# Two heads per score matmul and token-major values in a gated mix of linear and local attention

## The chip, the cores and the metric

The kernel runs on one core of a Trainium2 chip. Its time is device time in microseconds (us), and lower is better. The kernel before takes 492.45 us, the median of three runs (492.34 to 493.23). A core has a matrix engine (TensorE, PE in the profile, with its weight loads shown apart as PEld), a vector engine (VectorE, DVE), a scalar engine (ScalarE, ACT), a general engine (GpSimd, POOL) and a queue engine that only issues transfers (SyncE, SP). Matmul results land in PSUM, eight banks of 128 partitions by 512 fp32 columns; all other tiles lie in SBUF.

## The reference, cut to what matters

Sequence length S is 2048, width D is 1024, with 32 heads of 32 dimensions. One input x feeds two attention blocks, A and B, and a gate mixes their outputs.

```
def _A_ref(x, wqkv, wo):                     # linear attention
    phi = lambda t: jnp.where(t > 0, t + 1, jnp.exp(t)) + 1e-6
    pq, pk = phi(q), phi(k)
    kv = einsum("bhsd,bhse->bhde", pk, v);  z = einsum("bhsd->bhd", pk)
    o = einsum("bhqd,bhde->bhqe", pq, kv) / (einsum("bhqd,bhd->bhq", pq, z) + 1e-6)
    return o @ wo
def _B_ref(x, wqkv, wo):                     # local attention
    W, dil = 8, 2                            # each query sees positions s, s-2, ..., s-14
    logits = (q . k at those positions) * Dh ** -0.5, masked below position 0
    o = softmax(logits) weighted sum of v at those positions
    return o @ wo
g = sigmoid((x * gate_w).sum(-1))
out = g * A(x) + (1 - g) * B(x)
```

## The kernel before

Tokens are reordered into even and odd positions (`e_` is 0 or 1, 1024 tokens each, 16 tiles of 128 in all), so that the dilated window of local attention becomes eight neighbouring tokens. All activations are kept feature-major in SBUF: `xT`, `qT` and `kT` are [128, 8, 2048], eight chunks of 128 features, so a chunk `c` holds four heads `j` at 32 partitions each.

The stages, in order of time:

1. Values of B (L1370): each token tile times half of the value weights, token-major; a copy (`move`, on ACT or DVE) puts the 512 columns in a `vst` buffer, and SP writes them to `vB_hbm` in device memory.
2. Keys and queries of B (L1481), first for `e_` = 0, then for `e_` = 1, into `kT` and `qT`. `top` (L1287) keeps a running maximum and minimum of both on DVE.
3. Keys and values of A with the running state (`state`, L1511), token tile by token tile.
4. Queries of A, the state folded into A's output weights (`fold`), denominators (`over`), A's output (`a_out`), and at the end `final` (L1636), which multiplies `qT` (by then holding B's attention output) with B's output weights and mixes.

Local attention is cut into 18 fills, nine for each `e_`. A fill covers two blocks (`h` is 0 or 1) of 57 queries (56 in the last fill of nine), and each block needs the 64 keys before and at its queries. Fills are put between the projection groups of the second half of stage 2 and of stage 3: `slot` is called after each group, its rate of 0.2 (`FILL`) starts a fill every five groups, and `after(PVLAG, values)` puts the values three slots after the scores. In a fill, with four PSUM banks `SO` of its own:

- SP loads 64 token rows of `vB_hbm` for each block (L1411) into one of three `v` buffers.
- Scores (`s_fn`, L1418): for every chunk, block and head one matmul, 64 in all, with the 64 keys of the head as stationary operand (32 partitions by 64 columns) and 57 queries moving. Head `j` writes bank `j`, block `h` the partitions from 64`h`.
- ACT takes the exponential of all four banks into `E` (L1424), and DVE multiplies by a 0/1 mask (L1427).
- Values (`values`, L1432): for every head and block one matmul, 64 in all, with 64 tokens by 32 value columns as stationary operand and 57 columns of `E` moving; the result is feature-major. After `SUMS_AT` = 3 chunks, eight matmuls with `ones` as stationary operand give every head's sum, repeated over its 32 partitions (L1444).
- For each block ACT takes Ln of the sums (L1453) and the exponential of its negative (L1454), and DVE multiplies the result by it and overwrites the queries in `qT` (L1456).

The order of all instructions is made when the program is built: every `P.op` names its engine, an assumed cost, what it reads and writes, and a priority (its place in the program unless given). `schedule` is a list scheduler that goes through assumed time, gives each engine the ready operation of lowest priority number, and lets an operation marked `any` go to ACT or DVE, whichever would end it first. On PE it also prefers an operation of the same tile `mode` as the last. The result is a fixed order for each engine and for the SP queue, with semaphore waits where one engine needs another.

Of the kernel before, what the change touches and what calls it, by code (L numbers as in the profile page):

```python
# [1115 lines left out]
def build_kernel(nc, A_x, A_wqkv, A_wo, B_x, B_wqkv, B_wo, gate_w, out):  # L1116
# [10 lines left out]
    def SB(shape, dtype, name, at=None):  # L1127
        n = SZ[dtype]
        for d in shape[1:]:
            n *= d  # L1130
        if at is None:
            at = base[0]
            base[0] += (n + 31) // 32 * 32
        uid[0] += 1
        h = nc.alloc_sbuf_tensor_at("%s_%d" % (name, uid[0]), list(shape), dtype, offset=at)
        return Tile("S", h, at, list(shape), dtype)
# [26 lines left out]
            return ps[:, self.i, lo:hi]  # L1163

    banks = [Bank(i) for i in range(8)]
    vB_hbm = nc.dram_tensor("vB_hbm", [S, D], BF16)
    MX = [("M", 0, 1, None)]
    mx_hbm = nc.dram_tensor("mx_hbm", [4, 128], F32)
    rc_hbm = nc.dram_tensor("rc_hbm", [4, H, 4, 512], F32)
# [6 lines left out]
    kT = SB([128, 8, S], BF16, "kT")  # L1176
    ws = [SB([128, 8, 1024], BF16, "w%d" % i) for i in range(4)]
    pq0 = SB([128, 8, 512], BF16, "pq0")
    ones = SB([128, 32], BF16, "ones")
# [3 lines left out]
    msk = [SB([128, 2, n], BF16, "msk%d" % i) for i, (n, _) in enumerate(KINDS)]  # L1183
    eps = SB([128, 1], F32, "eps")
    gwb = SB([128, 1024], BF16, "gwb")
    gt = SB([128, NT], F32, "gt")
# [9 lines left out]
    er = Ring([SB([128, 512], BF16, "e%d" % i) for i in range(3)])  # L1196

    ph = base[0]
    vst = Ring([SB([128, 512], BF16, "vst%d" % i) for i in range(8)])
    top_ = base[0]  # L1200
    base[0] = ph
    Er = Ring([SB([128, 32 * 57], BF16, "E%d" % i) for i in range(2)])
    Lr = Ring([SB([128, 8 * 57], F32, "L%d" % i) for i in range(2)])
    vr = Ring([SB([128, 1024], BF16, "v%d" % i) for i in range(3)])
# [19 lines left out]

    FILL = 0.2
    PVLAG = 3
    SUMS_AT = 3
    WARM = 11
    PASSES = 6
    mm = lambda n: max(n / 2400.0, 0.0267) + 0.0025  # L1230
# [3 lines left out]
    def plan(seen):  # L1234
# [28 lines left out]
        C("pool", lambda e: e.memset(ones[:], 1.0), 0.1, [ones.all()])  # L1263
# [13 lines left out]
        C("pool", lambda e: e.memset(zsel[:], 0.0), 0.3, [zsel.all()])  # L1277

        C("dve", lambda e: e.memset(warm[:, :], 0.0), 0.15, [warm.all()])
        for m in mx[0:2]:  # L1280
            C("dve", lambda e, m=m: e.memset(m[:, :], 0.0), 0.2, [m.all()])

# [87 lines left out]
        for t, half in [(4 * b + i, half) for b in range(NT // 4) for half in range(2) for i in range(4)]:  # L1370
            vt, vs = vst.next()
            xs, xr = x_tile(t)
            bank = main.next()
            w, wr = w_half(0, half)
            step = 2 if t == 0 else 8
            for d in range(0, 8, step):
                o = group(bank, xs, w, [xr, ws[0].part((d, d + step), (half * 512, half * 512 + 512))], d, d + step)
            move(vt[:, :], bank.ap, 512, bank, vt.all())
            P.op("sp", lambda e, t=t, vt=vt, half=half: e.dma_start(vB_hbm[t * 128:(t + 1) * 128, half * 512:half * 512 + 512], vt[:, :]), 0.6, reads=[vt.all()],
                 writes=[hb(t * 128, (t + 1) * 128, half)], chan="vst%d" % vs, lat=0.5, prio=5)  # L1380
            if (t, half) in early:
                load_w(*early[t, half], after=[o])
# [19 lines left out]
        later = []  # L1402
        slot_n = [0]

        def fill(e_, qs, nq, offs):
            t0 = e_ * HS
            k0 = [qs + nq * h - offs[h] for h in range(2)]
            m = msk[KINDS.index((nq, offs))]
            vt, vslot = vr.next()
            for h in range(2):  # L1410
                P.op("sp", lambda e, h=h: e.dma_start(vt[64 * h:64 * h + 64, :], vB_hbm[t0 + k0[h]:t0 + k0[h] + 64, :]), 0.4,  # L1411
                     reads=[hb(t0 + k0[h], t0 + k0[h] + 64, i) for i in range(2)], writes=[vt.all()], chan="v%d_%d" % (vslot, h), lat=0.5)

            def s_fn(e):
                for c in range(8):
                    for h in range(2):
                        for j in range(4):
                            last = e.matmul(SO[j].ap(c * nq, (c + 1) * nq)[64 * h:64 * h + 64, :], kT[32 * j:32 * j + 32, c, t0 + k0[h]:t0 + k0[h] + 64],  # L1418
                                            qT[32 * j:32 * j + 32, c, t0 + qs + h * nq:t0 + qs + (h + 1) * nq], start=True, stop=True, tile_position=(32 * j, 64 * h))
                return last  # L1420
            P.op("pe", s_fn, 0.55, mode="r", reads=[kT.part((0, 8), (t0 + k0[0], t0 + k0[1] + 64)), qT.part((0, 8), (t0 + qs, t0 + qs + 2 * nq))],
                 writes=[s.iv for s in SO], name="S")
            E, _ = Er.next()
            P.op("act", lambda e: e.activation(E[:, 0:32 * nq].rearrange("p (j q) -> p j q", j=4), ps[:, 4:8, 0:8 * nq], ACT.Exp), act(32 * nq),  # L1424
                 reads=[s.iv for s in SO], writes=[E.all()])
            ev = lambda: E[:, 0:32 * nq].rearrange("p (g q) -> p g q", g=16)
            P.op("dve", lambda e: e.tensor_tensor(ev(), ev(), m[:, :, :].rearrange("p r q -> p (r q)")[:, None, :].to_broadcast([128, 16, 2 * nq]), ALU.mult),  # L1427
                 0.15 + 32 * nq / 1920.0, reads=[E.all(), m.all()], writes=[E.all()])

            def values():  # L1430

                def each(e):  # L1432
                    def part(c):
                        for j in range(4):
                            for h in range(2):
                                hd = 4 * c + j
                                last = e.matmul(SO[h].ap(c * nq, (c + 1) * nq)[32 * j:32 * j + 32, :], vt[64 * h:64 * h + 64, hd * 32:hd * 32 + 32],  # L1437
                                                E[64 * h:64 * h + 64, (8 * j + c) * nq:(8 * j + c + 1) * nq], start=True, stop=True, tile_position=(64 * h, 32 * j))
                        return last
                    for c in range(SUMS_AT):  # L1440
                        part(c)
                    for j in range(4):
                        for h in range(2):
                            e.matmul(SO[2 + h].ap(0, 8 * nq)[32 * j:32 * j + 32, :], ones[64 * h:64 * h + 64, :], E[64 * h:64 * h + 64, 8 * j * nq:8 * (j + 1) * nq],  # L1444
                                     start=True, stop=True, tile_position=(64 * h, 32 * j))
                    for c in range(SUMS_AT, 8):
                        last = part(c)
                    return last
                P.op("pe", each, 0.61, mode="c", reads=[vt.all(), ones.all(), E.all()], writes=[s.iv for s in SO], name="PV")
                for h in range(2):  # L1450
                    L, _ = Lr.next()
                    n = 8 * nq
                    P.op("act", lambda e, L=L, h=h: e.activation(L[:, 0:n], SO[2 + h].ap(0, n), ACT.Ln), act(n), reads=[SO[2 + h].iv], writes=[L.all()])  # L1453
                    P.op("act", lambda e, L=L: e.activation(L[:, 0:n], L[:, 0:n], ACT.Exp, scale=-1.0), act(n), reads=[L.all()], writes=[L.all()])  # L1454
                    q0 = t0 + qs + h * nq
                    P.op("dve", lambda e, L=L, h=h, q0=q0: e.tensor_tensor(  # L1456
                        qT[:, :, q0:q0 + nq], SO[h].ap(0, n).rearrange("p (c q) -> p c q", c=8), L[:, 0:n].rearrange("p (c q) -> p c q", c=8), ALU.mult), dps(n),
                        reads=[SO[h].iv, L.all()], writes=[qT.part((0, 8), (q0, q0 + nq))])
            after(PVLAG, values)

        pace = [0.0]

        states = []
# [308 lines left out]
```

## Time and profile before

| what | before |
|---|---|
| median of the runs | 492.45 us |
| the profiled execution, its own time | 492.7 us |
| its span, first to last instruction | 490.9 us |
| PE, DVE, ACT busy | 99%, 56%, 34% of the span |
| PE share of the chain that ended last | 95% |
| scores, all fills (L1418) | 1152 matmuls |
| values and sums, all fills (L1437, L1444) | 1152 and 144 matmuls |
| state (L1519) | 512 matmuls |
| Ln and exponential in a fill (L1453, L1454) | 548 and 584 ns each |
| DVE multiply into `qT` (L1456) | 628 ns each |

A share of busy time is an average over stages. The line of slices cuts the span in 40 equal parts, each digit the busy tenths of one. The chain of waits is followed back from the last instruction to whatever released each step. A line of the timeline gives start, length, engine, line of the kernel, operation, result and operands, tile and operand shape, and count; matmuls overlap, so the length of a group is the time from its first start to its last end. Fills lie between 126 and 312 us.

### The profile page before, as it was taken

What the parts mean: (1) busy time and instruction counts of PE and PEld (TensorE: products, weight loads), DVE (VectorE), ACT (ScalarE), POOL (GpSimd) and SP (SyncE); (2) the same over time, 40 slices, a digit from 0 to 9 for tenths busy, and PEclk for the clock granted to TensorE, in tenths of its full rate; (3) what the DMA queues carried; (4) which work ended last, traced back from release to release, by engine and by line L of the source; (5) the groups of instructions that cost most, each with busy time, mean ns of one, the idle gap of its engine ahead of it and who ended that gap; (6) DMA issues with size and microseconds to landing.
All of it is one profiled execution on the core that took longest, in us unless ns stands there. A gap on an engine that the chain in (4) does not pass through costs nothing.

```text
span 490.9 us, 11427 instructions
## 1 busy us (share of the span) xinstructions
PE 485.7 (99%) x5123; PEld 226.5 (46%) x5123; DVE 274.5 (56%) x487; ACT 166.9 (34%) x287; POOL 5.1 (1%) x27
## 2 busy tenths in 40 slices
PE   8999999999999999999999999999999999999997
PEld 3444444444444444555454454444444444444443
DVE  2121336899677777465555645596865735334434
ACT  2111121212443344665655556355423323010000
POOL 3000000000000000000000000000000000000000
PEclk9999999999999999999999999999999999999999
DMA  8999993222003045211000100501673406101212
GB/s 208 216 197 271 356 366 100 86 87 85 13 24 109 24 127 146 65 28 43 24 24 24 36 12 4 171 3 22 172 193 80 115 13 180 44 23 45 85 68 89
DMA packets 51069, 48.82 MB, mean 99 GB/s; under 512 B 20161, under 2 KB 38977, under 8 KB 51010
## 3 DMA queue, kind: packets, MB, share of 16 engines
q1 hardware_dynamic: 50322, 47.40, 34.9%
q8 instruction: 42, 0.69, 0.6%
q10 hardware_dynamic: 688, 0.59, 0.4%
q14 instruction: 17, 0.14, 0.1%
HBM read 34.34 MB, written 9.44 MB: 89 GB/s over the span
## 4 chain that ended last, share of the span: by engine, by line
PE 95%; SPq 2%; DVE 2%; DMA 1%; issue 0%
PE ps_all L1326 77%; PE ps_all L1647 11%; PE ps_all L1418 2%; PE ps_all L1437 2%; SPq L1300 1%; PE ps_all L1519 1%; DMA w<-in_B_wqkv_dram 1%; PE ps_all L1444 1%; DVE zsel L1561 1%; SPq L1305 1%; PE ps_all L1598 0%; DVE pq L1339 0%; PE ps_all L1571 0%; DVE e L1337 0%; DVE w L1357 0%
## 5 line engine op out<-in xcount | busy, mean ns | idle before, releaser
L1326 PE MATMUL ps_all<-w,xT 128*128 128x512 bf16 x960 | 213.8, 379 | 0.7 <-DMA xT<-in_A_x_dram 0.6
L1326 PE MATMUL ps_all<-xT,w 128*128 128x512 bf16 x768 | 170.7, 379 | 0.0
L1326 PEld LDWEIGHTS ps_all<-w,xT 128*128 128x128 bf16 x960 | 91.1, 98 | 109.8 <-DMA xT<-in_A_x_dram 2.0
L1326 PEld LDWEIGHTS ps_all<-xT,w 128*128 128x128 bf16 x768 | 73.8, 98 | 89.0 <-issue 1.8
L1647 PE MATMUL ps_all<-w,qT 128*128 128x512 bf16 (+1 forms) x264 | 55.6, 373 | 0.0
L1647 PEld LDWEIGHTS ps_all<-w,qT 128*128 128x128 bf16 x264 | 25.8, 98 | 29.7
L1337 DVE TENSOR_SCALAR e<-e 128x512 bf16<-128x512 bf16 x64 | 18.3, 290 | 34.3 <-ACT e L1335 17.1
L1357 DVE CAST vst<-ps_all 128x512 bf16<-128x512 f32 x15 | 10.4, 691 | 44.3 <-PE ps_all L1326 44.3
L1424 ACT ACTIVATE E<-ps_all 128x1824 bf16<-128x1824 f32 (+1 forms) x18 | 30.4, 1687 | 10.1 <-PE ps_all L1418 9.4
L1335 ACT ACTIVATE e<-ps_all 128x512 bf16<-128x512 f32 x32 | 19.1, 597 | 42.8 <-PE ps_all L1326 42.8
L1427 DVE TENSOR_TENSOR E<-E,msk 128x1824 bf16<-128x1824 bf16 (+1 forms) x18 | 19.8, 1102 | 22.4 <-ACT E L1424 22.4
L1651 DVE SCALAR_TENSOR_TENSOR o<-ps_all,gm,xT 128x512 bf16<-128x512 f32 (+1 forms) x25 | 18.0, 728 | 23.2 <-PE ps_all L1647 22.2
L1333 ACT ACTIVATE e<-ps_all 128x512 bf16<-128x512 f32 x32 | 19.1, 597 | 26.6 <-PE ps_all L1326 25.8
L1358 ACT ACTIVATE vst<-ps_all 128x512 bf16<-128x512 f32 x17 | 10.1, 597 | 49.7 <-PE ps_all L1326 45.5
L1287 DVE TENSOR_TENSOR mx<-mx,kT 128x1024 bf16<-128x1024 bf16 x32 | 20.8, 688 | 9.3 <-ACT kT L1358 9.2
L1287 DVE TENSOR_TENSOR mx<-mx,qT 128x1024 bf16<-128x1024 bf16 x32 | 20.8, 686 | 6.9 <-ACT qT L1361 6.7
L1456 DVE TENSOR_TENSOR qT<-ps_all,L 128x456 bf16<-128x456 f32 (+1 forms) x36 | 21.0, 627 | 6.2 <-ACT L L1454 5.0
L1339 DVE SCALAR_TENSOR_TENSOR pk<-ps_all,e 128x512 bf16<-128x512 f32 x32 | 21.9, 688 | 0.7
L1453 ACT ACTIVATE L<-ps_all 128x456 f32<-128x456 f32 (+1 forms) x36 | 17.8, 547 | 12.4 <-PE ps_all L1437 12.4
L1358 ACT ACTIVATE kT<-ps_all 128x512 bf16<-128x512 f32 x16 | 9.6, 597 | 34.5 <-PE ps_all L1326 34.5
L1361 ACT ACTIVATE qT<-ps_all 128x512 bf16<-128x512 f32 x16 | 9.6, 597 | 31.5 <-PE ps_all L1326 31.5
L1614 DVE TENSOR_TENSOR xT<-xT,rb 128x512 bf16<-128x512 bf16 x24 | 16.2, 688 | 6.6 <-DMA rb<-rc_hbm 6.4
(72 smaller groups left out, 285.6 us busy)
## 6 DMA issues: line engine op xcount, KB each, us to landing
rb<-rc_hbm SPq DMA_DIRECT2D x32, 256.0 KB, 4.8
w<-in_A_wqkv_dram SPq DMA_DIRECT2D x6, 1024.0 KB, 9.3
v<-vB_hbm SPq DMA_DIRECT2D x36, 128.0 KB, 2.8
vB_hbm<-vst SPq DMA_DIRECT2D x32, 128.0 KB, 5.9
w<-in_B_wqkv_dram SPq DMA_DIRECT2D x4, 1024.0 KB, 9.5
xn<-in_A_x_dram SPq DMA_DIRECT2D x16, 256.0 KB, 2.8
out_dram<-o SPq DMA_DIRECT2D x15, 256.0 KB, 2.0
w<-in_A_wo_dram SPq DMA_DIRECT2D x8, 256.0 KB, 3.9
```

Source lines behind the costliest of these rows:

```text
L1287: P.op("dve", lambda e, m=m, op=op: e.tensor_tensor(m[:, 0:n], m[:, 0:n], src, op), 0.08 + n / 1920.0, reads=[m.all(), reg], writes=[m.all()],
L1326: last = e.matmul(bank.ap(), lhs(dc), rhs(dc), start=(dc == 0), stop=(dc == 7))
L1333: P.op("act", lambda e: e.activation(e_[:, :], bank.ap(), ACT.Exp), act(512), reads=[bank.iv], writes=[e_.all()])
L1335: P.op("act", lambda e: e.activation(e_[:, :], bank.ap(), ACT.Exp, accum_out=qe[:, col:col + 1]), act(512) + 0.1, reads=[bank.iv], writes= ...
L1337: P.op("dve", lambda e: e.tensor_scalar(e_[:, :], e_[:, :], 1.0, 1e-6, op0=ALU.min, op1=ALU.add), 0.25, reads=[e_.all()], writes=[e_.all()])
L1339: P.op("dve", lambda e: e.scalar_tensor_tensor(out=dst, in0=bank.ap(), scalar=0.0, in1=e_[:, :], op0=ALU.max, op1=ALU.add), dps(512), read ...
L1358: fa = lambda e: e.activation(dst, src(), ACT.Copy)
L1424: P.op("act", lambda e: e.activation(E[:, 0:32 * nq].rearrange("p (j q) -> p j q", j=4), ps[:, 4:8, 0:8 * nq], ACT.Exp), act(32 * nq), rea ...
L1427: P.op("dve", lambda e: e.tensor_tensor(ev(), ev(), m[:, :, :].rearrange("p r q -> p (r q)")[:, None, :].to_broadcast([128, 16, 2 * nq]), ...
L1456: P.op("dve", lambda e, L=L, h=h, q0=q0: e.tensor_tensor(qT[:, :, q0:q0 + nq], SO[h].ap(0, n).rearrange("p (c q) -> p c q", c=8), L[:, 0:n ...
L1647: last = e.matmul(bank.ap(0, f1 - f0), qT[:, dc, t * 128:(t + 1) * 128], ws[3][:, dc, f0:f1], start=(dc == 0), stop=(dc == 7))
L1651: P.op("dve", lambda e, bank=bank, o_=o_, t=t, n=n, i0=i0, i1=i1, tgt=tgt, c0=c0: e.scalar_tensor_tensor(out=o_[:, i0 * 128:i1 * 128].rear ...
```

## The change

- **Scores.** A masked copy `qd` of the fill's queries is built first by two operations (ACT or DVE): copy `k` = 0 keeps the even heads of a chunk and zeroes the odd ones, `k` = 1 the reverse, by a factor `par` of 1 or 0 per partition. One matmul then takes 64 partitions of keys (two heads) as stationary operand and both copies (2 x 57 columns) as moving operand: 32 matmuls in place of 64. The scores now come two slots after the fill's start (`after(2, ...)`), the values three slots after them.
- **Values.** The stored rows of `vB_hbm` have 33 columns per head, the last one set to 1 in the `vst` buffers once. `E` is now the stationary operand (64 tokens by 57 queries) and the 33 columns of a head move, so the result is token-major, 57 queries of a block by 32 values and the sum. The eight `ones` matmuls and `SUMS_AT` go. The results lie in all four banks.
- **Division.** For each block one DVE reciprocal of the 16 sums per partition and one DVE multiply from PSUM into a token-major buffer `ot`; ACT's Ln and exponential go.
- **Way back.** Four SP writes per fill put `ot` into `oB_hbm`, and as soon as all rows of a token tile are written, one SP transfer with transpose puts the tile back into `qT`, 16 in all.
- Buffers: `qd` lies where `pq0` is used later; `L` goes; `ot`, `rs` and the wider `v` rows lie over the `vst` buffers of stage 1.

```diff
-    vB_hbm = nc.dram_tensor("vB_hbm", [S, D], BF16)
+    vB_hbm = nc.dram_tensor("vB_hbm", [S, 33 * H], BF16)
+    oB_hbm = nc.dram_tensor("oB_hbm", [S, D], BF16)
...
+        for z in vst.t:
+            C("pool", lambda e, z=z: e.memset(z[:, :, 32:33], 1.0), 0.1, [z.part((0, 16), (32, 33))])
...
+        for j in range(4):
+            for k in range(2):
+                C("dve", lambda e, j=j, k=k: e.memset(par[32 * j:32 * j + 32, k:k + 1], 1.0 if j % 2 == k else 0.0), 0.1, [par.all()])
+                P.ops[-1].prio = 1100
...
-            move(vt[:, :], bank.ap, 512, bank, vt.all())
+            move(vt[:, :, 0:32], lambda bank=bank: bank.ap().rearrange("p (h d) -> p h d", d=32), 512, bank, vt.part((0, 16), (0, 32)))
...
+        def place(hd):
+
+            c, j = hd // 4, hd % 4
+            return 8 * (2 * (j // 2) + c // 4) + 2 * (c % 4) + j % 2
...
+            Q, _ = qd.next()
+            for k in range(2):
+                src = qT[:, :, t0 + qs:t0 + qs + 2 * nq]
+                fd = lambda e, k=k: e.tensor_scalar(Q[:, :, k, 0:2 * nq], src, par[:, k:k + 1], None, op0=ALU.mult)
+                fa = lambda e, k=k: e.activation(Q[:, :, k, 0:2 * nq], src, ACT.Copy, scale=par[:, k:k + 1])
+                P.op("any", {"act": fa, "dve": fd}, {"act": act(16 * nq), "dve": 0.15 + 16 * nq / 1920.0}, reads=[qT.part((0, 8), (t0 + qs, t0 + qs + 2 * nq)), par.all()],
+                     writes=[Q.part((0, 8), (k, k + 1), (0, 114))])
...
-                        for j in range(4):
-                            last = e.matmul(SO[j].ap(c * nq, (c + 1) * nq)[64 * h:64 * h + 64, :], kT[32 * j:32 * j + 32, c, t0 + k0[h]:t0 + k0[h] + 64],
-                                            qT[32 * j:32 * j + 32, c, t0 + qs + h * nq:t0 + qs + (h + 1) * nq], start=True, stop=True, tile_position=(32 * j, 64 * h))
+                        for r in range(2):
+                            c0 = 2 * (c % 4) * nq
+                            last = e.matmul(SO[2 * r + c // 4].ap(c0, c0 + 2 * nq)[64 * h:64 * h + 64, :], kT[64 * r:64 * r + 64, c, t0 + k0[h]:t0 + k0[h] + 64],
+                                            Q[64 * r:64 * r + 64, c, :, h * nq:(h + 1) * nq], start=True, stop=True, tile_position=(64 * r, 64 * h))
                 return last
...
+            after(2, lambda: rest(e_, qs, nq, t0, k0, m, vt, Q, s_fn))
...
+                    for i in range(16):
+                        for w in range(2):
+                            hd = 16 * w + i
                             for h in range(2):
-                                hd = 4 * c + j
-                                last = e.matmul(SO[h].ap(c * nq, (c + 1) * nq)[32 * j:32 * j + 32, :], vt[64 * h:64 * h + 64, hd * 32:hd * 32 + 32],
-                                                E[64 * h:64 * h + 64, (8 * j + c) * nq:(8 * j + c + 1) * nq], start=True, stop=True, tile_position=(64 * h, 32 * j))
...
+                                c = 33 * (i % 8)
+                                g_ = place(hd)
+                                last = e.matmul(SO[2 * h + i // 8].ap(c, c + 33)[64 * w:64 * w + nq, :], E[64 * h:64 * h + 64, g_ * nq:(g_ + 1) * nq],
+                                                vt[64 * h:64 * h + 64, hd * 33:hd * 33 + 33], start=True, stop=True, tile_position=(64 * h, 64 * w))
...
-                P.op("pe", each, 0.61, mode="c", reads=[vt.all(), ones.all(), E.all()], writes=[s.iv for s in SO], name="PV")
+                P.op("pe", each, 0.55, mode="c", reads=[vt.all(), E.all()], writes=[s.iv for s in SO], name="PV")
+                o, os_ = ot.next()
                 for h in range(2):
...
-                    P.op("act", lambda e, L=L, h=h: e.activation(L[:, 0:n], SO[2 + h].ap(0, n), ACT.Ln), act(n), reads=[SO[2 + h].iv], writes=[L.all()])
-                    P.op("act", lambda e, L=L: e.activation(L[:, 0:n], L[:, 0:n], ACT.Exp, scale=-1.0), act(n), reads=[L.all()], writes=[L.all()])
...
+                    P.op("dve", lambda e, r=r, bv=bv: e.reciprocal(r[:, :].rearrange("p (k i) -> p k i", k=2), bv()[:, :, :, 32:33].rearrange("p k i c -> p k (i c)")), 0.2,
+                         reads=two, writes=[r.all()])
+                    P.op("dve", lambda e, r=r, bv=bv, h=h: e.tensor_tensor(
+                        o[:, 512 * h:512 * h + 512].rearrange("p (k i c) -> p k i c", k=2, c=32), bv()[:, :, :, 0:32],
+                        r[:, :].rearrange("p (k i) -> p k i", k=2)[:, :, :, None].to_broadcast([128, 2, 8, 32]), ALU.mult), dps(512),
+                        reads=two + [r.all()], writes=[o.part((512 * h, 512 * h + 512))])
+                q0 = t0 + qs
+                for w, (r0, r1) in [(w, r_) for w in range(2) for r_ in ((0, 48), (48, nq))]:
+                    P.op("sp", lambda e, w=w, r0=r0, r1=r1: e.dma_start(
+                        oB_hbm[q0:q0 + 2 * nq, 512 * w:512 * w + 512].rearrange("(h q) f -> q h f", h=2)[r0:r1], o[64 * w + r0:64 * w + r1, :].rearrange("p (h f) -> p h f", h=2)), 0.5,
+                        reads=[o.all()], writes=[[("O%d_%d" % (w, r0), q0, q0 + 2 * nq, None)]], chan="oo%d_%d_%d" % (os_, w, r0), lat=0.3)
+                while rows[0] < NT and q0 + 2 * nq >= 128 * (rows[0] + 1):
+                    t, rows[0] = rows[0], rows[0] + 1
+                    P.op("sp", lambda e, t=t: e.dma_start_transpose(qT[:, :, t * 128:(t + 1) * 128], oB_hbm[t * 128:(t + 1) * 128, :]), 1.5,
+                         reads=[[("O%d_%d" % (w, r0), t * 128, (t + 1) * 128, None)] for w in range(2) for r0 in (0, 48)], writes=[qT.part((0, 8), (t * 128, (t + 1) * 128))], chan="ot%d" % t, lat=1.3)
```

More of the change, by code (lines that the diff above doesn't have):

```diff
@@ L1178, in build_kernel @@
     pq0 = SB([128, 8, 512], BF16, "pq0")
-    ones = SB([128, 32], BF16, "ones")
     FILLS = [(2 * 57 * b, 57, (0 if b == 0 else 7, 7)) for b in range(8)] + [(2 * 57 * 8, 56, (7, 8))]
@@ L1183, in build_kernel @@
     msk = [SB([128, 2, n], BF16, "msk%d" % i) for i, (n, _) in enumerate(KINDS)]
+    qd = Ring([SB([128, 8, 2, 114], BF16, "qd%d" % i, at=pq0.lo + 4096 * i) for i in range(2)])
+    par = SB([128, 2], F32, "par")
     eps = SB([128, 1], F32, "eps")
@@ L1198, in build_kernel @@
     ph = base[0]
-    vst = Ring([SB([128, 512], BF16, "vst%d" % i) for i in range(8)])
+    vst = Ring([SB([128, 16, 33], BF16, "vst%d" % i) for i in range(8)])
     top_ = base[0]
@@ L1202, in build_kernel @@
     Er = Ring([SB([128, 32 * 57], BF16, "E%d" % i) for i in range(2)])
-    Lr = Ring([SB([128, 8 * 57], F32, "L%d" % i) for i in range(2)])
-    vr = Ring([SB([128, 1024], BF16, "v%d" % i) for i in range(3)])
+    ot = Ring([SB([128, 1024], BF16, "ot%d" % i) for i in range(2)])
+    rs = Ring([SB([128, 16], F32, "rs%d" % i) for i in range(4)])
+    vr = Ring([SB([128, 33 * H], BF16, "v%d" % i) for i in range(3)])
     mtmp = [SB([128, 2, 57], BF16, "mt%d" % i, at=vr.t[2].lo + 256 * i) for i in range(2)]
@@ L1226, in build_kernel @@
     PVLAG = 3
-    SUMS_AT = 3
     WARM = 11
@@ L1261, in C @@
             return P.op(eng, fn, cost, reads=reads, writes=writes, prio=-1)
-        C("pool", lambda e: e.memset(ones[:], 1.0), 0.1, [ones.all()])
+        for z in vst.t:
+            C("pool", lambda e, z=z: e.memset(z[:, :, 32:33], 1.0), 0.1, [z.part((0, 16), (32, 33))])
         C("pool", lambda e: e.memset(eps[:], 1e-6), 0.1, [eps.all()])
@@ L1377, in plan @@
                 o = group(bank, xs, w, [xr, ws[0].part((d, d + step), (half * 512, half * 512 + 512))], d, d + step)
-            move(vt[:, :], bank.ap, 512, bank, vt.all())
-            P.op("sp", lambda e, t=t, vt=vt, half=half: e.dma_start(vB_hbm[t * 128:(t + 1) * 128, half * 512:half * 512 + 512], vt[:, :]), 0.6, reads=[vt.all()],
+            move(vt[:, :, 0:32], lambda bank=bank: bank.ap().rearrange("p (h d) -> p h d", d=32), 512, bank, vt.part((0, 16), (0, 32)))
+            P.op("sp", lambda e, t=t, vt=vt, half=half: e.dma_start(vB_hbm[t * 128:(t + 1) * 128, half * 528:half * 528 + 528], vt[:, :, :].rearrange("p h d -> p (h d)")), 0.6, reads=[vt.all()],
                  writes=[hb(t * 128, (t + 1) * 128, half)], chan="vst%d" % vs, lat=0.5, prio=5)
@@ L1416, in s_fn, with rest @@
                     for h in range(2):
-                        for j in range(4):
-                            last = e.matmul(SO[j].ap(c * nq, (c + 1) * nq)[64 * h:64 * h + 64, :], kT[32 * j:32 * j + 32, c, t0 + k0[h]:t0 + k0[h] + 64],
-                                            qT[32 * j:32 * j + 32, c, t0 + qs + h * nq:t0 + qs + (h + 1) * nq], start=True, stop=True, tile_position=(32 * j, 64 * h))
-                return last
-            P.op("pe", s_fn, 0.55, mode="r", reads=[kT.part((0, 8), (t0 + k0[0], t0 + k0[1] + 64)), qT.part((0, 8), (t0 + qs, t0 + qs + 2 * nq))],
-                 writes=[s.iv for s in SO], name="S")
+                        for r in range(2):
+                            c0 = 2 * (c % 4) * nq
+                            last = e.matmul(SO[2 * r + c // 4].ap(c0, c0 + 2 * nq)[64 * h:64 * h + 64, :], kT[64 * r:64 * r + 64, c, t0 + k0[h]:t0 + k0[h] + 64],
+                                            Q[64 * r:64 * r + 64, c, :, h * nq:(h + 1) * nq], start=True, stop=True, tile_position=(64 * r, 64 * h))
+                return last
+            after(2, lambda: rest(e_, qs, nq, t0, k0, m, vt, Q, s_fn))
+        def rest(e_, qs, nq, t0, k0, m, vt, Q, s_fn):
+            P.op("pe", s_fn, 0.46, mode="r", reads=[kT.part((0, 8), (t0 + k0[0], t0 + k0[1] + 64)), Q.all()], writes=[s.iv for s in SO], name="S")
             E, _ = Er.next()
@@ L1432, in each @@
                 def each(e):
-                    def part(c):
-                        for j in range(4):
+                    for i in range(16):
+                        for w in range(2):
+                            hd = 16 * w + i
                             for h in range(2):
-                                hd = 4 * c + j
-                                last = e.matmul(SO[h].ap(c * nq, (c + 1) * nq)[32 * j:32 * j + 32, :], vt[64 * h:64 * h + 64, hd * 32:hd * 32 + 32],
-                                                E[64 * h:64 * h + 64, (8 * j + c) * nq:(8 * j + c + 1) * nq], start=True, stop=True, tile_position=(64 * h, 32 * j))
-                        return last
@@ L1440, in each @@
[L1440 to L1447, printed above, removed]
@@ L1450, in values @@
+                    return last
+                P.op("pe", each, 0.55, mode="c", reads=[vt.all(), E.all()], writes=[s.iv for s in SO], name="PV")
+                o, os_ = ot.next()
                 for h in range(2):
-                    L, _ = Lr.next()
-                    n = 8 * nq
-                    P.op("act", lambda e, L=L, h=h: e.activation(L[:, 0:n], SO[2 + h].ap(0, n), ACT.Ln), act(n), reads=[SO[2 + h].iv], writes=[L.all()])
-                    P.op("act", lambda e, L=L: e.activation(L[:, 0:n], L[:, 0:n], ACT.Exp, scale=-1.0), act(n), reads=[L.all()], writes=[L.all()])
@@ L1455, in values @@
[L1455 to L1458, printed above, removed]
+                    r, _ = rs.next()
+                    bv = lambda h=h: ps[:, 4 + 2 * h:6 + 2 * h, 0:264].rearrange("p k (i c) -> p k i c", c=33)
@@ new lines, in values @@
+                    two = [SO[2 * h].iv, SO[2 * h + 1].iv]
+                    P.op("dve", lambda e, r=r, bv=bv: e.reciprocal(r[:, :].rearrange("p (k i) -> p k i", k=2), bv()[:, :, :, 32:33].rearrange("p k i c -> p k (i c)")), 0.2,
[4 more added lines that the diff above has]
+                        reads=two + [r.all()], writes=[o.part((512 * h, 512 * h + 512))])
@@ L1459, in fill @@
+                while rows[0] < NT and q0 + 2 * nq >= 128 * (rows[0] + 1):
+                    t, rows[0] = rows[0], rows[0] + 1
+                    P.op("sp", lambda e, t=t: e.dma_start_transpose(qT[:, :, t * 128:(t + 1) * 128], oB_hbm[t * 128:(t + 1) * 128, :]), 1.5,
+                         reads=[[("O%d_%d" % (w, r0), t * 128, (t + 1) * 128, None)] for w in range(2) for r0 in (0, 48)], writes=[qT.part((0, 8), (t * 128, (t + 1) * 128))], chan="ot%d" % t, lat=1.3)
             after(PVLAG, values)
+        rows = [0]
```

## The prediction

> **What bounds the kernel.** I read the page's busy rows and slices first, then the chain of waits, then the groups by line and shape, and last the starts of single matmuls in the trace.
>
> ```profile
> span 490.9 us, 11427 instructions
> PE 485.7 (99%) x5123; PEld 226.5 (46%) x5123; DVE 274.5 (56%) x487; ACT 166.9 (34%) x287; POOL 5.1 (1%) x27
> PE   8999999999999999999999999999999999999997
> DVE  2121336899677777465555645596865735334434
> ACT  2111121212443344665655556355423323010000
> PEclk9999999999999999999999999999999999999999
> PE 95%; SPq 2%; DVE 2%; DMA 1%; issue 0%
> ```
>
> TensorE (PE) is busy in every slice at a full clock and holds 95% of the chain, so a microsecond taken out of PE's stream shortens the program by a microsecond, and work on DVE, ACT or a queue counts only when PE has to wait for it. The windows of the two stages that run the local attention say how much cover there is:
>
> ```profile
> core 0: us, PE busy (x) PEld busy (x) DVE busy (x) ACT busy (x) POOL busy (x), PEclk, DMA share, GB/s
> 122.00:192.00 70.00, 70.00 (x1030) 33.67 (x1027) 51.05 (x82) 28.78 (x43) 0.31 (x2) 1.00 0.26 73
> 192.00:312.00 120.00, 120.00 (x2628) 61.10 (x2628) 66.84 (x120) 69.50 (x105) 0.00 (x0) 1.00 0.11 29
> ```
>
> PE has no idle time there; DVE is busy 73% and 56%, ACT 41% and 58%. The local attention itself (one fill: scores, then values) is this in PE's timeline, 18 times:
>
> ```profile
> 138.43 0.70 PE L1418 MATMUL ps_all<-qT,kT 32*64 32x57 bf16 x64
> 139.06 0.39 PE L1326 MATMUL ps_all<-xT,w 128*128 128x512 bf16 x1
> ...
> 144.34 0.28 PE L1437 MATMUL ps_all<-E,v 64*32 64x57 bf16 x24
> 144.44 0.38 PE L1444 MATMUL ps_all<-E,ones 64*32 64x456 bf16 x8
> 144.63 0.51 PE L1437 MATMUL ps_all<-E,v 64*32 64x57 bf16 x40
> 145.07 0.39 PE L1326 MATMUL ps_all<-xT,w 128*128 128x512 bf16 x1
> ...
> 264.11 0.38 PE L1519 MATMUL ps_all<-az,pk 128*32 128x33 bf16 x32
> 264.43 0.39 PE L1326 MATMUL ps_all<-w,xT 128*128 128x512 bf16 x1
> ```
>
> From first start to the next projection matmul: scores 635 ns, values 727 ns. Inside them the single starts show a pattern. The scores' first 32 matmuls come in rounds of 8 (one on each tile), a round every 32 ns; then 98 ns nothing; the other 32 start every 8.33 ns; the last one is followed by the next projection after 140 ns. In the values, rounds of 8 come every 29 ns, the eight sums hold PE 190 ns, late matmuls again start every 8.33 ns, and 128 ns follow the last start. The state's 32 matmuls (L1519) come in rounds of 4 every 25 ns, with 110 ns after the last. So there are two prices: about 32 matmuls are already queued and run at the array's pace, and what follows comes at 8.33 ns each, 237 ns after the first at the earliest.
>
> **The array's pace.** A round is 32 ns with a 64-column weight load and 57 moving columns, 29 with 32 and 57, 25 with 32 and 33. The longer of the two, at 2.4 columns per ns, plus 5.5 ns fits the first two (26.7 + 5.5, 23.75 + 5.5), with 25 ns as the least seen.
>
> **Scores after (gain).** 64 matmuls of 57 columns become 32 of 114, four tiles of 64x64, so 8 rounds of 4. All 32 fit in what is queued: no 98 ns gap, no 8.33 ns part. A round is 114/2.4 + 5.5 = 53 ns; the last start is 7 x 53 + 10 = 381 ns after the first; the tail of 140 ns grows with the columns, by up to 24 ns, and I take 150. Sum 531 ns against 635: **-104 ns**. Bounds: rounds of 50 and tail 140 give 500; rounds of 60 and tail 165 give 595.
>
> **Values after (gain).** The eight sums go (their columns ride as the 33rd column of each head), and E becomes the stationary operand: 64 matmuls, 57-column loads, 33 moving columns, 16 rounds of 4. A round costs 57/2.4 + 5.5 = 29 ns, so the first 32 take 8 x 29 = 234 ns, about when the 33rd can come (237). The remaining 31 steps at 8.33 take 258. Last start 495, tail 125: 620 against 727: **-107 ns**.
>
> Here the Trainium skill speaks against the change. "TensorE: Matmul & The Clock Gate", section "LDWEIGHTS (loading the stationary operand)", prices a load at its columns over 1.2 per ns. 57 columns would be 47.5 ns a round (an estimate from that page): 15 x 47.5 + 10 + 125 = 848 ns, 121 more than now, which would eat the scores' gain: 18 x (121 - 104) = +0.3 us in all. The row says otherwise: the scores of before load 64 columns on each tile every 32 ns, which 53 ns a load does not allow unless loads of one tile overlap. I take the row; a load and its matmul not overlapping at all on one tile (23.75 + 13.75 + 5.5 = 43 ns) is my upper bound, 15 x 43 + 10 + 125 = 780, +53 ns.
>
> **Order on PE.** Entering another tile shape costs 309 - 216 = 93 ns over the projection's own step, twice per fill, as now. But 13 of the 16 state blocks now stand directly beside values and share that switch. With scores two slots later the cadence of fills moves against the states' four; I expect 2 or 3 of these pairs to part: **+0.2 us** (0 to 0.6).
>
> **DVE and ACT (at nothing).** Per fill ACT loses two Ln and two Exp, 2 x (548 + 584) = 2.26 us, and DVE two multiplies of 628 ns. Added: two reciprocals of 128x16, nearest row L1395 at 241 ns; two multiplies of 512, 628 + 56 x 1 = 684 ns; two masked copies of 912 bf16 elements on either engine. On DVE the nearest row, L1337, has 290 ns for 512, so at most 517 each; on ACT L1361 with a scale has 686 for 512, and 400 more elements at 0.833 ns (from 597 and 1690) make 1.02 us. If DVE takes both copies it gains 1.85 + 1.03 - 1.26 = 1.6 us per fill and ACT loses 2.3. Six groups per fill in the first stage (11.9 us, DVE 8.6) leave 1.7 us; should fills come every five groups, DVE has 6.3 x 5/6 + 1.1 + 1.85 + 1.03 = 9.2 of 10 us, and ACT has over 5 us free for the copies. Without that cover, every fill would pay the excess on PE.
>
> **The new wait.** Scores now wait for their copies, and behind them in PE's stream stand all later projections. The copies wait only for qT (written long before) and for a buffer that scores two fills earlier read, so they may run a fill ahead. At nothing.
>
> **Queues (at nothing).** Per fill SP gains four writes (0.45 to 0.58 us to issue each, by the rows of vst and v) and 16/18 of a transpose (1.29 us, row L1300, 4.1 us to landing): 2.0 + 1.15, with the two v loads 0.89: 4 us of every 9 to 12. A transpose waits for the writes (v's rows 2.8 us, vst's 5.9 in the crowded stage), holding what stands behind it: later v loads, which have three buffers and a fill's length to land, and weight loads needed after 318 us. The last transpose lands near 322; the first reader of these columns:
>
> ```profile
> L1647 PE MATMUL ps_all<-w,qT x264: 272/379/379, 418.5 to 487.5; 128*128 128x512 bf16 x124, 128*128 128x256 bf16 x8
> ```
>
> That is 96 us of cover. The value rows of 1056 instead of 1024 bytes add 3% to writes that cost PE nothing (ACT waited once, 4.2 us, PE none). The memsets of vst's columns and par stand on POOL and DVE in the first stage, where both are nearly idle.
>
> **Sum.** 18 x (0.104 + 0.107) = 3.8, less 0.2: **-3.6 us**. The profiled execution had 490.9 of span in 492.7 us; I expect a span near 487.3, hence 489.1 for such an execution and 492.45 - 3.6 = **488.9 us** against the median. Bounds of the two stages (scores 500 to 595, values 600 to 780) give -4.7 to +0.2 us.
>
> **Rivals.**
> (a) *Part of the gain only* (0.15): loads and matmuls of one tile don't overlap, values get 53 ns slower, scores gain 40 to 104: between -0.9 us and +0.2, so 491.5 to 492.7. For it: no 64x64 tile with a 57-column load is in the trace. Against: the 32 ns rounds.
> (b) *PE waits for the copies at the scores* (0.10, slower): place, PE at the scores of each fill; DVE runs at 73% and the planned cost of a copy (0.63 us on DVE, 0.95 on ACT) may be short. It decides from 3.6/18 = 0.2 us a fill; at 0.5 us a fill it gives +9 - 3.6 = 497.9. Against: copies run ahead, and the real PE blocks are longer than their planned 0.55 and 0.61 us, which gives other engines time.
> (c) *Four tiles share the moving rows*, so the two column tiles of a row group go in turn (0.03): 16 rounds of 53, 18 x (15 x 53 + 10 + 150 - 635) = +5.8 us, slower. Against: 8 tiles of two column groups overlap today.
> (d) *The gain is larger* (0.10): rounds of 50, fewer switches: -4.7 us, 487.7.
>
> **Numbers.** My own forecast has 0.62, from 488.0 to 490.2. What the measurement can tell from no change is 0.2%, 1 us. Faster by more: mine, (d) and a third of (a): 0.77; within 0.2%: the rest of (a), 0.10; slower: (b) and (c), 0.13. Leaving out the far half of each side, the range is 487.4 to 491.8.
>
> **What would show it.** Right: scores' 32 matmuls with starts in fours every 50 to 56 ns and no gap, 0.53 us to the next projection; values 0.62 us with no 190 ns hold; PE without idle time between 122 and 320 us. Wrong: PE idle before the scores with DVE or ACT named as releaser; starts of the values' fours every 43 ns or more; PE waiting for qT after 418 us; many more switches than 18 + 18 + 3.

## The result and the profile after

The changed kernel takes 487.88 us (median of four runs, 487.6 to 488.11) against 492.57 us, a ratio of 0.9902 with a 95% interval of 0.9885 to 0.9919. Run again beside other kernels it took 488.5 us against 492.44, 0.9922 (0.9908 to 0.9935). The forecast was 488.9 us in a range of 487.4 to 491.8. The profiled execution has 486.2 us of span in 488.11 us.

The page after, in the same rows as before:

```profile
span 486.2 us, 10107 instructions
PE 474.9 (98%) x4336; PEld 222.2 (46%) x4403; DVE 288.4 (59%) x557; ACT 139.0 (29%) x225; POOL 5.5 (1%) x34
PE   8999999999999999999999999999999999999997
DVE  2112336899788888575666656596865735434444
ACT  2111111214322233324534333455423322010000
PEclk9999999999999999999999999999999999999999
PE 95%; DVE 2%; issue 1%; DMA 1%; SPq 0%; ACT 0%; DVEq 0%
```

PE is still the bound, at the same clock. Its 98% is not idle time: the page counts 4336 matmuls but 4403 weight loads, so 67 matmul records are missing. Where single blocks are timed below, I therefore use the starts of weight loads, which are all there in both traces. ACT lost 28 us of work and DVE gained 14.

The windows of the two stages with fills, after:

```profile
core 0: us, PE busy (x) PEld busy (x) DVE busy (x) ACT busy (x) POOL busy (x), PEclk, DMA share, GB/s
122.00:192.00 70.00, 68.41 (x879) 33.29 (x892) 57.22 (x107) 22.02 (x27) 0.24 (x1) 1.00 0.42 110
192.00:312.00 120.00, 117.15 (x2036) 58.85 (x2061) 76.35 (x161) 47.39 (x59) 0.00 (x0) 1.00 0.33 83
```

DVE is busy 82% and 64% and the DMA engines 42% and 33% (26% and 11% before); both had the room. One fill in PE's timeline, after (the gap of 0.16 before the last line is a missing record):

```profile
139.14 0.60 PE L1439 MATMUL ps_all<-qd,kT 64*64 64x114 bf16 x32
139.67 0.39 PE L1333 MATMUL ps_all<-xT,w 128*128 128x512 bf16 x1
...
144.96 0.68 PE L1462 MATMUL ps_all<-v,E 64*57 64x33 bf16 x64
145.80 0.38 PE L1333 MATMUL ps_all<-xT,w 128*128 128x512 bf16 x1 [0.16 <-issue]
```

The scores last 533 ns to the next projection, where they took 635. The single starts in the trace come in fours: 78 ns from the first four to the second, then 51 ns each, no pause. In the values, fours come every 29.5 ns (52 for the first), and from about the 48th matmul on one every 8.33 ns (the weight loads, which run ahead, from about the 38th); the 190 ns of the sums are gone.

To see where the time went, the traces are cut by PE's own work: the starts of 128x128 weight loads, eight to a projection group, counted from the first group. All 18 fills lie between the 32nd and the 160th group.

| kernel | start of group 32 | 32 to 160 (fills) | 160 to 168 | 168 to 192 | 192 to 256 |
|---|---|---|---|---|---|
| before | 62.30 | 254.19 | 15.77 | 43.97 | 110.41 |
| before, second trace | 61.65 | 254.17 | 15.78 | 44.92 | 110.41 |
| after | 61.50 | 250.45 | 15.78 | 43.87 | 110.41 |
| after, second trace | 61.85 | 250.44 | 15.77 | 43.88 | 110.41 |

The change is 3.73 us in the stretch with the fills and nothing behind it. The rest of the first measurement's 4.7 us is not the change's work. In its two traces 0.8 us of it lies ahead of group 32 and 0.1 between groups 168 and 192. The start of group 32 spreads over 1.3 us among the traces of this case, and the stretch from 168 to 192, where PE stands before the denominators until DVE has their operand, over 1 us; both vary in the kernel before as well. The five times of the repeat (488.15 to 488.89) all lie above the four of the first measurement, with the same stretch of fills (250.44 us). In the two traces 0.35 us of it is a later group 32; what moved the whole set of runs is not known.

### The profile page after: what moved, and what is told of

It reads as the page before. It is cut to its first block, busy times and chain, and to the rows that moved or that the text cites. A ratio compares the mean times of both kernels' runs of the same rounds, so it can differ in the third digit from the quotient of the medians.

```text
span 486.2 us, 10107 instructions
## 1 busy us (share of the span) xinstructions
PE 474.9 (98%) x4336; PEld 222.2 (46%) x4403; DVE 288.4 (59%) x557; ACT 139.0 (29%) x225; POOL 5.5 (1%) x34
## 4 chain that ended last, share of the span: by engine, by line
PE 95%; DVE 2%; issue 1%; DMA 1%; SPq 0%; ACT 0%; DVEq 0%
PE ps_all L1333 78%; PE ps_all L1675 11%; PE ps_all L1462 2%; PE ps_all L1439 2%; DMA xT<-in_A_x_dram 1%; PE ps_all L1547 1%; DVE zsel L1589 1%; PE ps_all L1626 0%; DVE pq L1346 0%; SPq L1307 0%; PE ps_all L1599 0%; SPq L1312 0%; DVE rs L1471 0%; DVE e L1344 0%; ACT e L1340 0%
## 5 line engine op out<-in xcount | busy, mean ns | idle before, releaser
L1333 PE MATMUL ps_all<-w,xT 128*128 128x512 bf16 x921 | 209.1, 379 | 4.6 <-issue 1.9
L1333 PE MATMUL ps_all<-xT,w 128*128 128x512 bf16 x747 | 168.3, 379 | 2.0 <-issue 1.3
L1364 DVE CAST vst<-ps_all 128x512 bf16<-128x512 f32 x15 | 10.4, 694 | 43.1 <-PE ps_all L1333 43.1
L1365 ACT ACTIVATE az<-ps_all 128x512 bf16<-128x512 f32 x22 | 13.2, 599 | 38.3 <-PE ps_all L1333 38.3
L1365 ACT ACTIVATE vst<-ps_all 128x512 bf16<-128x512 f32 x17 | 10.2, 599 | 47.5 <-PE ps_all L1333 47.5
L1473 DVE TENSOR_TENSOR ot<-ps_all,rs 128x512 bf16<-128x512 f32 x36 | 23.6, 683 | 0.2 <-DVE rs L1471 0.2
```

The costliest lines, as they stand in the source:

```text
L1333: last = e.matmul(bank.ap(), lhs(dc), rhs(dc), start=(dc == 0), stop=(dc == 7))
L1473: P.op("dve", lambda e, r=r, bv=bv, h=h: e.tensor_tensor(o[:, 512 * h:512 * h + 512].rearrange("p (k i c) -> p k i c", k=2, c=32), bv()[:, ...
```

## The experiments

Times are medians; "fills" is the stretch from group 32 to group 160 (254.2 before, 250.4 after). A block is timed from its first weight load to the first projection load behind it. An entry is a step from a projection into a small tile shape.

**Scores alone.** The kernel before with the new `fill` and `s_fn`; the old values read their heads in the new order:

```diff
-   E[64 * h:64 * h + 64, (8 * j + c) * nq:(8 * j + c + 1) * nq]
+   E[64 * h:64 * h + 64, (16 * (j // 2) + 2 * c + j % 2) * nq:(16 * (j // 2) + 2 * c + j % 2 + 1) * nq]
```

> The scores of the change (masked copies, 32 matmuls of 114 columns, two slots later) with the values, sums, division and qT of the kernel before; the sums' moving operand picks its head out of the new order of E. My theory: 533 ns for the scores instead of 635, 18 x 0.102 = 1.8 us faster, near 490.7 us; values stay at 727 ns. Rival (a gain of order and cover, not of the matmul blocks): the two parts alone don't add up to the 4.7 us of the whole, this one gives under 1 us.

Measured: 492.1 us, ratio 0.9994 (0.9985 to 1.0003), though the scores block fell from 632 to 531 ns as forecast. The gain was given back at one place. The waits of PE's weight loads and its timeline, scores alone:

```profile
PEld ps_all L1588 <- ACT w L1364: 1.8, 1, 1.8
...
318.01 0.27 PE L1454 MATMUL ps_all<-E,v 64*32 64x56 bf16 x24
318.11 0.38 PE L1461 MATMUL ps_all<-E,ones 64*32 64x448 bf16 x8
318.30 0.50 PE L1454 MATMUL ps_all<-E,v 64*32 64x56 bf16 x40
318.96 5.13 PE L1332 MATMUL ps_all<-xT,w 128*128 128x512 bf16 x23 [0.16 <-issue]
324.02 0.43 PE L1588 MATMUL ps_all<-w,kvT 32*32 32x512 bf16 x16
326.01 0.44 PE L1588 MATMUL ps_all<-w,kvT 32*32 32x512 bf16 x16 [1.55 <-DVE w L1363]
```

The last values come at 318 us, past the 160th group, and two folds then stand side by side in the fixed order, so that the second waits for the copies of the first. From group 160 to 168 this kernel takes 18.12 us, not 15.77: 0.8 us of the excess is the last values block with its entry, the other 1.5 the stall. Why the plan put two folds together was not tried apart. (The fills' stretch, 251.73, lacks that block, which has slipped behind its end.)

**Scores alone, without the lag.** The same kernel with its scores at the fill's start:

```diff
-            after(2, lambda: rest(e_, qs, nq, t0, k0, m, vt, Q, s_fn))
+            (lambda f: f())(lambda: rest(e_, qs, nq, t0, k0, m, vt, Q, s_fn))
```

> The scores alone again, but placed at the fill's start instead of two slots later. In the run with the lag PE stood 1.8 us before the second fold, behind DVE's copies of the first, and the last values came at 318 us. Theory A (the lag, with the old and longer division, pushes the last fill into the fold's DVE work): last values near 312 us, no stall at the fold, 1.8 us faster than before, near 490.7 us. Theory B (the stall comes with the new scores): the stall stays, 492 us.

Measured: 490.48 us, ratio 0.9963 (0.9949 to 0.9976), fills 252.45 (-1.7), 160 to 168 back at 15.77, last values at 312.7 us:

```profile
312.73 0.19 PEld L1454 LDWEIGHTS ps_all<-E,v 64*32 64x32 bf16 x24
```

Theory A holds for the lag: without it the stall is gone and the score blocks give their 1.8 us. That the old, longer division is what makes the lag harmful is argued, not shown: the changed kernel has the lag and no stall (its last values start at 309.5 us), but it differs in its values and its way back too.

**Values alone.** The changed kernel with the old `s_fn` at the fill's start, without the masked copies and the lag, and with `place` returning `8 * j + c`:

> The values of the change (33 columns a head, E as stationary operand, reciprocal on DVE, way back over device memory) with the 64 score matmuls of the kernel before. My theory: 624 ns for the values instead of 727, 18 x 0.103 = 1.85 us, near 490.7 us; scores stay at 635 ns. Rival: under 1 us, as above.

Measured: 490.41 us, ratio 0.9959 (0.9946 to 0.9972). The values block takes 611 ns (726 before). Fills 252.94, a gain of 1.2: 18 x 0.115 = 2.1 us from the blocks, 0.1 back for one more entry into a small tile, 0.3 for three score blocks of about 740 instead of 632 ns, and some 0.5 at a single stop in the middle of the first state block:

```profile
194.77 0.27 PE L1536 MATMUL ps_all<-az,pk 128*32 128x33 bf16 x15
195.35 0.28 PE L1536 MATMUL ps_all<-az,pk 128*32 128x33 bf16 x17 [0.30 <-issue]
```

The trace names nothing that these matmuls waited for, so the cause of the stops stays open. The forecast of the block and of the run's time (490.7) hold; the stops were not foreseen.

**The kernel before without its sums.**

```diff
-                    for j in range(4):
-                        for h in range(2):
-                            e.matmul(SO[2 + h].ap(0, 8 * nq)[32 * j:32 * j + 32, :], ones[64 * h:64 * h + 64, :], ...)
...
-   e.activation(L[:, 0:n], SO[2 + h].ap(0, n), ACT.Ln)
+   e.activation(L[:, 0:n], SO[2 + h].ap(0, n), ACT.Exp)
```

> The kernel before without the eight sum matmuls of a fill (its output is not the reference's: the first of ACT's two steps reads what the scores left in the bank, as an exponential). Theory A, the values gain comes from the eight sums alone and the 64 matmuls cost the same in either operand order because the 33rd and later come at 8.33 ns: 237 + 258 + 128 = 623 ns, 1.9 us faster than before. Theory B, the exchanged operands matter too: the old order stays well above 623 ns (the sums' place filled by other gaps), under 1.2 us faster.

Measured: 489.91 us, ratio 0.9953 (0.9941 to 0.9966); fills 251.97, -2.2. The weight loads of one values block, without sums and in the kernel before:

```profile
132.11 0.57 PEld L1437 LDWEIGHTS ps_all<-E,v 64*32 64x32 bf16 x64 [0.42 <-DVE mx L1287]
132.72 0.55 PEld L1326 LDWEIGHTS ps_all<-xT,w 128*128 128x128 bf16 x4
```

```profile
144.34 0.17 PEld L1437 LDWEIGHTS ps_all<-E,v 64*32 64x32 bf16 x24 [0.42 <-DVE mx L1287]
144.42 0.11 PEld L1444 LDWEIGHTS ps_all<-E,ones 64*32 64x32 bf16 x8
144.47 0.56 PEld L1437 LDWEIGHTS ps_all<-E,v 64*32 64x32 bf16 x40
145.06 0.11 PEld L1326 LDWEIGHTS ps_all<-xT,w 128*128 128x128 bf16 x2
```

132.11 to 132.72 is 607 ns, less than the 612 of the new values. So theory A: all of the values' gain is the eight sum matmuls. Exchanging the operands, with the 33rd column, costs 5 ns; it earns its place by making the sum that column.

**Scores in 64 halves.** The changed kernel, each score matmul cut in two:

```diff
-   last = e.matmul(... SO[...].ap(c0, c0 + 2 * nq) ..., Q[64 * r:64 * r + 64, c, :, h * nq:(h + 1) * nq], ...)
+   for k in range(2):
+       last = e.matmul(... SO[...].ap(c0 + k * nq, c0 + (k + 1) * nq) ..., Q[64 * r:64 * r + 64, c, k, h * nq:(h + 1) * nq], ...)
```

> The changed kernel with each of the 32 score matmuls cut in two (one for each masked copy), 64 of 57 columns on the same four tiles, the same columns in all. Theory A (the number of matmuls sets the price once 32 are queued): 32 in rounds of about 32 ns, then 8.33 ns each, 650 to 680 ns instead of 533, 2.1 to 2.6 us slower than the changed kernel, near 490.2 us. Theory B (moved columns set it): no more than 0.5 us slower.

Measured: 491.69 us, ratio to before 0.9993 (0.9982 to 1.0004); fills 253.41, 3.0 us more than the changed kernel. One block's weight loads here and in the changed kernel:

```profile
139.69 0.65 PEld L1440 LDWEIGHTS ps_all<-qd,kT 64*64 64x64 bf16 x64 [0.42 <-issue]
140.38 0.11 PEld L1333 LDWEIGHTS ps_all<-xT,w 128*128 128x128 bf16 x2
```

```profile
139.14 0.45 PEld L1439 LDWEIGHTS ps_all<-qd,kT 64*64 64x64 bf16 x32 [0.42 <-issue]
139.67 0.11 PEld L1333 LDWEIGHTS ps_all<-xT,w 128*128 128x128 bf16 x2
```

684 ns against 531 with the same columns, the same tiles and the same copies, a little more than forecast (650 to 680), and 3.0 us in the fills where 2.1 to 2.6 were; three blocks took 40 to 110 ns longer than the others. The number of matmuls sets the price, not the columns: the change moves twice as many and gains. But this run does not tell why a matmul more costs time here. Its first 32 come in fours every 32 ns, 8 ns each, and the others take 9.1 ns each, so on four tiles the first pace and the later one are nearly the same. Sixteen rounds of 32 ns where the changed kernel has eight of 51 are 102 ns more by themselves, of 153. That the 33rd and later come slowly is seen where eight tiles work: in the kernel before, 32 scores start within 139 ns, then none for 98 ns, then one every 8.33. That the first 32 are queued and the others fed is the reading of those starts; no record shows a queue.

**No way back.** The changed kernel without the four `oB_hbm` writes of a fill and the 16 transposes:

> The changed kernel without the four writes of a fill and without the 16 transposes; qT keeps the queries, so the output is not the reference's. My theory (the way back is hidden by 96 us): within 0.5 us of the changed kernel. Rival (these transfers hold back v loads, or their reads of device memory cost PE): 1 us or more faster.

Measured: 488.68 us, and 488.5 for the changed kernel beside it; fills 250.44. Hidden, as forecast.

**Copies twice.**

```diff
-            for k in range(2):
+            for k in (0, 1, 0, 1):
                 src = qT[:, :, t0 + qs:t0 + qs + 2 * nq]
```

> The changed kernel with each masked copy made twice, four operations a fill, the same result. My theory (copies run ahead under cover of DVE and ACT, 0.45 us each more on DVE, 0.9 us a fill): within 0.4 us of the changed kernel. Rival (PE's scores wait for the copies): 18 x up to 0.9 us, up to 16 us slower, and 1.8 us slower at the least if a tenth of a microsecond a fill is uncovered.

Measured: 488.9 us (488.23 to 489.51), beside 488.5 (488.15 to 488.89) for the changed kernel; fills 250.45, not 0.02 us more, so the 0.4 us between the medians is not from the fills. The scheduler put 21 of the 72 copies on ACT (1.05 us each) and 51 on DVE (0.45). PE waits for none.

**No lag in the changed kernel.** The edit of the second experiment, on the changed kernel:

> The changed kernel with its scores at the fill's start. If the copies run ahead as I argued, PE doesn't wait for them: within 0.4 us of the changed kernel, and no idle time at the scores in the trace. If the lag of two slots is what hides the copies: over 1 us slower, with the copies named as what ended PE's waits.

Measured: 488.81 us, ratio 0.9926 (0.9913 to 0.994), fills 250.34. The two slots are not what hides the copies: a fill's second copy ends 7.0 to 21.8 us before its scores here, and 10.4 to 20.1 us in the changed kernel.

**The changed kernel again, and the kernel before again.**

> The changed kernel again beside the others of this call: 487.9 us. Its first 15 us tell whether PE's start, 0.8 us earlier than before in the first profile, belongs to the change: if it does, the 32nd projection group starts near 61.5 us again; if it is the scatter of the first transfers, anywhere from 61 to 62.5.

> The kernel before again, for its first 15 us and for the stage of the fills: 492.4 us; the stretch from the 32nd to the 160th projection group 254.2 us as in its first profile; the 32nd group anywhere between 61.5 and 62.8 us if PE's start is scatter of the first transfers.

Measured: 488.5 and 492.5 us; group 32 at 61.85 and 61.65 us, fills 250.44 and 254.17. The changed kernel's time came 0.6 us over its forecast, the fills of both within 0.02 us of their first traces: the start moves from execution to execution, the fills do not.

**One tile mode name.** A try at a better version:

```diff
-            P.op("pe", s_fn, 0.46, mode="r", ...)
+            P.op("pe", s_fn, 0.46, mode="c", ...)
```

> The changed kernel with the scores under the same tile mode name as values and state, so that the list scheduler puts a ready state block beside them: entries from a projection into a small tile shape fall from 41 to 37 in the fixed order. My theory: 4 x 93 ns, 0.4 us faster than the changed kernel, if a state block behind scores saves the entry as one behind values does. Rival: leaving the 64x64 shape of the scores costs as much as leaving the projection, no gain.

> The version with one tile mode name again: 0.4 us faster than the changed kernel, and 250.0 us between the 32nd and the 160th projection group (250.4 in the changed kernel).

Measured: 488.31 and 488.37 us, ratios to before 0.9918 (0.9905 to 0.9932) and 0.9909 (0.9894 to 0.9924), beside 0.9922 and 0.9902 for the changed kernel. In the order six state blocks now follow scores; entries fall to 37. Fills take 250.03 and 250.04 us, 0.41 less, for four entries fewer, and settle that a state block behind scores saves what one behind values saves:

```profile
191.48 0.45 PEld L1439 LDWEIGHTS ps_all<-qd,kT 64*64 64x64 bf16 x32 [0.42 <-issue]
192.01 0.27 PEld L1547 LDWEIGHTS ps_all<-az,pk 128*32 128x32 bf16 x32
```

The run times can't tell 0.4 us from none.

## Why the prediction was right

**The sum.** It had 3.8 us of shorter blocks less 0.2 of order, -3.6; the stretch with the fills shows -3.73. By weight loads, scores went from 632.5 to 531 ns and values from 726 to 612: 18 x (0.1015 + 0.114) = 3.88. Entries from a projection into a small tile went from 39 to 41, as two of the 13 paired state blocks parted: +0.19. That is -3.69. Two small terms close the rest: by what the loads show, a parted pair costs 108 ns and not 93, and the two pairs that have the state block first took 37 ns more each before and do not now: -3.88 + 0.22 - 0.07 = -3.73.

The number for the whole owes something to luck. The first median, 487.88 us, is 1.0 below the forecast and just outside my own 488.0 to 490.2; the fills gave 3.73 of the 4.69 us, and the rest lies outside them. The repeat, 488.5, is inside.

**Scores.** Forecast 531 ns from matmul start to matmul start, measured 533. The parts were off both ways: a later round took 51 ns, not 53, the first took 78, which I had not seen coming (in the kernel before the first round is drawn out too, 53 ns against 32), and the tail 141, not 150. The halved scores show that the number of matmuls was the right thing to count.

**Values.** Forecast 620, measured about 624 (500 to the last start, some 124 behind it). Rounds of 29.5 and then 8.33 ns were as forecast, though the change from one to the other came later than the 33rd matmul and mattered little: at 29.5 ns to the end the last start would have been at 475 ns. Loads at 1.2 columns per ns, as the Trainium skill's page "TensorE: Matmul & The Clock Gate" has them in "LDWEIGHTS (loading the stationary operand)", would have shown as rounds of 47.5 ns, an estimate from that page; the trace disagrees, and so rival (a), rounds of 43 ns with loads and matmuls of one tile in turn, falls too. What I had not said is that the gain is the eight sums alone.

**At nothing.** Copies: nearest row scaled gave at most 517 ns on DVE and 1.02 us on ACT; they took 450 and 1049. Reciprocal and multiply: 241 and 684 forecast, 234 and 683 measured. Fills of the first stage did come every five groups, 10.0 us apart (11.9 before), and DVE was busy 8.2 of these 10 us, not the 9.2 of my sum. The copies done twice (rival (b)) and the way back left out both changed nothing in the fills. The way back was a little cheaper than thought in issue, with one exception, in the source view of its transposes, after:

```profile
L1484 SPq DMA_TRANSPOSE qT<-oB_hbm x16: 1237/1242/5046, 156.5 to 318.8; - x16
```

One issue took 5.05 us, at 308 us, right behind two 1 MB weight loads; the last left at 318.8 us and the first reader of `qT` comes at 413.7, so it cost nothing.

**Rival (c)**, column tiles in turn, would have shown as 16 rounds of 53 ns in the scores; there are eight of 51. The larger gain of rival (d), 487.7 us, is near the first median by what lies outside the fills, not by its mechanism: the rounds of 51 ns were paid back by the first one, and switches rose.

**What I left out.** The parts are not independent, and the prediction treated the two-slot lag as free. In the changed kernel it is; with the old values and division the scores alone with the lag gained nothing.

## What to carry to other kernels

Where small matmuls run in short blocks inside a stream of large ones, count instructions before columns: in the scores of the kernel before, 32 ran at the array's pace, and every further one cost 8.33 ns, so that halving the number was worth doubling the columns. Price a block by its rounds from the nearest tile shapes in the trace, and add the entry and the tail (93 and 110 to 141 ns here); letting two small blocks stand side by side saved some 0.1 us of this a pair. Judge a change of this size by the stretch of one engine's own work in the trace, since the scatter of the start alone was a third of the gain, and try each part alone, because an order fixed at build time can give a part's gain back somewhere else.

## What was not expected of the hardware

- The first round of a block is drawn out: 78 ns before the second one in the scores, 51 later; 52 and 29.5 in the values.
- A weight load of 64 columns and one of 57 both kept a tile's round near 30 ns (32 and 29.5), with 57 or 33 columns moving in it. Load and matmul of one tile overlap there: in a block of the scores before, the second matmuls of the tiles start 53 ns after the first and the third loads from 58 ns on, while 57 columns take 24 ns by the projections' 216 ns for 512.
- With 64 score matmuls on four tiles the block cost 684 ns, with 64 on eight tiles 632: the fours of 57 columns come every 32 ns and the 33rd matmul starts after 281 ns, while on eight tiles it starts after 237.
- The start of the 32nd projection group moved between 61.5 and 62.8 us from execution to execution, in kernels whose PE work up to there is alike.
